# A Fourier filter in front of a gated feed-forward layer: inverse transforms of three y tiles in one unit instead of two

## The chip, the cores and the metric

The kernel runs on one core of one Trainium2 chip. Times are device microseconds (us) of one execution; the kernel before was run three times, and its time is the median of these.

## What is computed

A batch of 8 sequences (3008 tokens, 256 features, 32-bit floats) is filtered in frequency space, and each token then goes through a two-layer network with a hard-swish gate:

```python
X = np.fft.rfft(x, axis=1)                      # x: (8, 3008, 256)
Y = X * (filt_r + 1j * filt_i)[None]
y = np.fft.irfft(Y, n=3008, axis=1).reshape(24064, 256)
h = y @ w_in                                    # 256 -> 2048
g = h * np.clip(h + 3.0, 0.0, 6.0) / 6.0
out = g @ w_out                                 # 2048 -> 256
```

## The kernel before

**The network sets the rhythm.** Tokens are taken in 47 blocks of 512 (`k`), hidden features in 8 parts of 256 (`p`). One pair (k, p) is one **step**; step i is 8k + p, and there are 376. Both matrix products are done in Strassen's way with 7 products. In step i the loop emits the up product of (k, p) and, woven into it, the down product of the step before, (kd, pd):

1. `up_1`: three products into the PSUM banks `al` and `be`;
2. `do(0)`: the place for EARLY units of the transform;
3. `g_sums`: on VectorE (DVE), the second half of the gate of the step before (`hswish(.., 1)`, L737) and the sums L744, L745, L747; then down product 1;
4. `up_2`: two products. If pd is 0, `out_4` on DVE (L838, L839), which reads bank `po2` of the last block. Then `up_2b`: DVE adds h = be + s (L713), after which `be` is not used until the next step;
5. down products 2 and 4; if pd is 7, `out_1` (ScalarE, L820); `up_3`: one product into `al`, then DVE L718, which reads `al`; down products 5 and 6;
6. `up_4`: the first relu on ScalarE (L732); `do(1)`: the place for `w_scale`;
7. if pd is 0, `out_5` on DVE (L843), which reads bank `po3` of the last block; `hswish(.., 0)` on DVE (L737);
8. `up_5`: the last up product into `al`; ScalarE copies it (L727) and does the second relu (L732);
9. if pd is 7, `out_2` and `out_3` on DVE (L829, L834) around down products 7 and 3; `do(2)`: the place for all other units.

At p = 0 new `po` tiles are taken in the same four PSUM banks: in the step with pd = 0, down product 5 is the first that writes `po2`, and down product 7 the first that writes `po3`.

**The transform is threaded through the steps.** A batch n is transformed while the blocks before it go through the network. Its units are given to steps by hand, with lists in `places(n)`, and a unit's instructions run in the order of the code: each engine takes its instructions in this order (the schedule is manual). For n = 2 to 7 the steps are counted here from a base of 8·first[n] − 40, written as +j (first[n] is 11, 17, 23, 29, 35, 41):

- `a_unit` (L446): first transform, in +j below zero and again from +34 on for the next batch;
- `b_unit` (L493): second transform of two tiles, in both banks `psf`, at +2, +6, +12, +18, +22, +28, EARLY;
- `f_unit`: filter products, three DVE operations (L514 to L516), at +2, +3, +6, +7, +12, +13 and 16 steps later, in `do(2)`;
- `y_unit`: two DVE operations (L525, L526) that finish a y tile, at +4, +5, +10, +11, +14, +15 and 16 later, in `do(2)`; three buffers (`yp`);
- `bi_unit`: first inverse transform of two y tiles, EARLY, at +8, +14, +17, +24, +30, +33. Four products of 64 rows, 64 columns and 512 elements (L537), each on another quarter of the TensorE array, into the two banks of the pool `psF`; two ScalarE copies (L540) into `t3`; then `g_store`, two DMAs from the GpSimd queue (L553), in `do(2)`;
- `n_five` and `n_unit` (L627, L638): the last inverse transform, EARLY, most often at +1, +9, +16, +25; both banks of `psF`. ScalarE copies the tokens into `xn`, and after some of them `t_sums` on GpSimd (L683) makes the sums that the up product takes.

Each 32-bit product is two instructions in the records.

Of the kernel before, what the change touches and what calls it, by code (L numbers as in the profile page):

```python
# [10 lines left out]
FP32 = mybir.dt.float32  # L11
I32 = mybir.dt.int32
AXT = mybir.ActivationFunctionType
# [19 lines left out]
P = 128  # L33
D = 256
# [147 lines left out]
def kernel(  # L182
# [9 lines left out]
    nc = tc.nc  # L192
# [12 lines left out]
    g_d = nc.dram_tensor("g_tmp", (B, NC, 2, KH, D), FP32, kind="Internal").ap()  # L205
# [3 lines left out]
    def pool(name, bufs, **kw):  # L209
        return ctx.enter_context(tc.tile_pool(name=name, bufs=bufs, **kw))  # L210

    const = pool("const", 1)
    t1p = pool("t1p", 2)
# [3 lines left out]
    t3p = pool("t3p", T3B)  # L217
# [6 lines left out]
    psF = pool("psF", 2, space=PSUM)  # L224
    psU = pool("psU", 1, space=PSUM)
# [10 lines left out]
    wi = const.tile([P, 4, NC], FP32, name="wi")  # L236
# [10 lines left out]
    st = {}  # L247
# [282 lines left out]
    def bi_unit(b, i, ps=None):  # L530
        ys = [st.pop(("y", b, i + v)) for v in range(2)]
        ps = ps or [psF.tile([P, 2, D], FP32, name="psf", tag="f") for ri in range(2)]
        for v, ri in ((0, 0), (1, 0), (0, 1), (1, 1)):

            products = isinstance(ys[v], tuple)
            w, y = (wi[:, 1 + ri, :], ys[v][ri]) if products else (wi[ts(ri, 64), 0 if b else 3, :], ys[v][ts(ri, 64)])
            nc.tensor.matmul(ps[ri][ts(v, 64)], w, y, start=True, stop=True)  # L537
        t = (t3p if b or i & 2 else t1p).tile([P, 2, 2, D], FP32, name="t3" if b or i & 2 else "t1")
        for ri in range(2):
            nc.scalar.activation(out=t[:, ri, :, :], in_=ps[ri], func=AXT.Copy)  # L540
        st["t3", b, i] = t

    def g0_first(i):
        t = st["t3", 0, i]
        for v in range(2):
            for h in range(2):
                (nc.scalar, nc.sync)[v].dma_start(g_d[0, ds(h * HC + 1, NJ + 1), :, ds(2 * (i + v), 2), :].rearrange("c ri u d -> c ri (u d)"),
                                    t[ds(v * 64 + h * HC + 1, NJ + 1)].rearrange("p ri u d -> p ri (u d)"))
# [10 lines left out]
    for b in range(B):  # L559
# [4 lines left out]
        n = 0  # L564
# [106 lines left out]
    def xb(k, d, c):  # L671
        return xn[:, d, c, ts(k % 3, PAIRS)]
# [13 lines left out]
    def product(ps, p, w, x, start=False, stop=False):  # L686
        nc.tensor.matmul(ps, w_in[p][:, w, :], x, start=start, stop=stop, skip_group_check=True)  # L687
# [36 lines left out]
    def up_5(k, p):  # L724
        al = st["up"][0]
        product(al, p, A22, xb(k, 1, 1), stop=True)
        nc.scalar.activation(out=st["h"][1][:, 0:256], in_=al, func=AXT.Copy)  # L727
        relu(1)

    def relu(i):  # L730
        r = rp.tile([P, 512], FP32, name="r", tag="r")
        nc.scalar.activation(out=r, in_=st["h"][i], func=AXT.Relu, bias=half_c, scale=1.0 / 6.0)  # L732
        st["r", i] = r
# [56 lines left out]
    def plain_up(p):  # L790
        st["g", 0, p] = gp.tile([P, 7, 256], FP32, name="g")
        st["h"] = [psU.tile([P, 512], FP32, name=n) for n in ("al", "be")]
        for i in range(2):
            for d in range(2):
                nc.tensor.matmul(st["h"][i], w_in[p][:, 2 * d + i, :], xn[:, d, :, 0:PAIRS], start=d == 0, stop=d == 1)  # L795
            relu(i)
            hswish(0, p, i)

    def plain_down(p, tokens=(0, 1)):
        g = st["g", 0, p]  # L800
        if p == 0:
            st["po", 0] = [psO.tile([P, 2, 2, P], FP32, name="po%d" % i) for i in range(2)]
        for t in tokens:
            for u in range(2):
                for i, a in ((0, G11), (1, G12)):
                    nc.tensor.matmul(st["po", 0][t][:, u, :, :].rearrange("p a m -> p (a m)"), g[:, a + t, ts(u, P)],  # L806
                                     w_out[p][:, 2 * i:2 * i + 2, :].rearrange("p j m -> p (j m)"),
                                     start=p == 0 and u == 0 and i == 0, stop=p == NP - 1, skip_group_check=True)
# [50 lines left out]
    for b in range(B):  # L859
        for n, m, na in (((0, 6, NA), (6, 16, NA), (22, 9, NA)) if b == 0 else ((0, 16, NA), (16, 15, NA)) if b < B - 1  # L860
                         else ((0, 16, NA), (16, 10, NA), (26, 1, SPLIT))):
            o = b * HC * NA + n * NA
# [27 lines left out]
    plan = {}  # L890


    EARLY = (a_unit, b_unit, bi_unit, n_unit, n_five)

    def at(step, fn, *a):
        plan.setdefault((step, 0 if fn in EARLY else 1 if fn == w_scale else 2), []).append((fn, a))

    with tc.manual_schedule():

# [42 lines left out]
        ps = psU.tile([P, 512], FP32, name="al")  # L942
# [115 lines left out]
        def places(n):  # L1058
            if n == 1:
                return (list(range(2, NB + 2)), [12, 13, 15, 18, 19, 20, 22, 23, 26, 27, 28, 30],  # L1060
                        [14, 15, 16, 19, 21, 22, 24, 25, 27, 29, 30, 31], [16, 21, 24, 29, 31, 32])
            k = first[n] * NP
            a_at = [k - 7 * NP + i for i in (2, 4, 7, 9, 11, 13, 14, 15)]
            f_at, y_at, bi_at = ([k - (5 - 2 * r) * NP + i for r in range(2) for i in p]
                                 for p in ((2, 3, 6, 7, 12, 13), (4, 5, 10, 11, 14, 15), (8, 14, 17)))
            return a_at, f_at, y_at, bi_at

        at(n_at[TAIL - 2] + 1, lambda: nc.sync.dma_start(edge, wai_d[:, ds(NW + ND, ND)]))
# [2 lines left out]
        for n in range(1, B):  # L1071
            a_at, f_at, y_at, bi_at = places(n)
            for c, s in enumerate(a_at):
                at(s, a_unit, n, c)
                at(s, a_sums, n, c)
                at(s, z_store, n, c, nc.sync if n == 1 else nc.gpsimd)
                if c >= 3:
                    at(max(a_at[c - 3], s - 6), x_load, n, c)
                elif n > 1:
                    at(max(prev[c + NB - 3], s - 6), x_load, n, c)  # L1080
            for c in range(NT):
                s = f_at[2 * (c - TB) + (n == 1)] + 1 if c >= TB else a_at[-1] + 1
                at(s, t2_load, n, c)
                s = f_at[2 * (c - FB) + 1] + 1 if c >= FB else a_at[-1 if n > 1 else 3] + 1
                at(s, table_load, n, c)
            for i in range(NU):
                if i % 2 == 0 or n == 1:
                    at(f_at[i], b_unit, n, i)
                if i % 2 == 0:
                    at(bi_at[i // 2], bi_unit, n, i)  # L1090
                    at(bi_at[i // 2], g_store, n, i)
                at(y_at[i], y_unit, n, i)
            for i in range(NU):
                at(f_at[i], f_unit, n, i)
            prev = a_at
# [4 lines left out]
        for i in range(len(items) + 1):  # L1100
            up = i < len(items)
            k, p = items[min(i, len(items) - 1)]
            dn = i > 0
            kd, pd = items[i - 1]
            def do(place):
                for fn, a in plan.get((i, place), ()):
                    fn(*a)

            if k == 0:
                plain_up(p)  # L1110
                do(0)
                if dn:
                    plain_down(pd)
                do(1)
                do(2)
                continue
            if not up:
                last_down()
                break
            up_1(k, p)  # L1120
            ends = k == LAST and p == NP - 1
            do(0)
            last_plain = dn and kd == 0
            dn = dn and kd > 0
            if dn:
                g_sums(kd, pd)
                down(kd, pd, 1)
            if up:
                up_2(k, p)
            if dn and pd == 0 and kd > 1:  # L1130
                out_4(kd - 1)
            if up:
                up_2b(k, p)
            if dn:
                down(kd, pd, 2, 4)
                if pd == NP - 1:
                    out_1(kd)
            if up:
                up_3(k, p)
            if dn:  # L1140
                down(kd, pd, 5, 6)
            if up:
                up_4(k, p)
                do(1)
            if ends:
                out_1(k)
            if last_plain:
                plain_down(pd, (0,))
            if dn and pd == 0 and kd > 1:
                out_5(kd - 1)  # L1150
            if up:
                hswish(k, p, 0)
            if up:
                up_5(k, p)
            if last_plain:
                plain_down(pd, (1,))
                plain_out()
            if dn:
                if pd == NP - 1 or ends:
                    out_2(kd)  # L1160
                down(kd, pd, 7, 3)
                if pd == NP - 1 or ends:
                    out_3(kd)
            do(2)
# [30 lines left out]
```

## Time and profile before

| | us |
|---|---|
| median of 3 runs | 2660.61 (2660.59 to 2660.66) |
| the profiled execution's own time | 2658.29 |
| its span, first to last instruction | 2656.3 |
| PE busy | 2640.7 (99%) |
| DVE busy | 2053.4 (77%) |
| ScalarE (ACT) busy | 1318.7 (50%) |
| GpSimd (POOL) busy | 495.6 (19%) |

The views used are the page (busy time, the chain of work that ended last), the waits (who waited for whom), one engine's timeline (start and duration in us, engine, line, operation, out<-in, count, and in brackets the idle time before with what ended it) and the groups by line. PE is TensorE's matmuls, PEld its weight loads. A step is measured from the first matmul of its `up_1` to the next step's. All timelines are on the span's clock.

### The profile page before, as it was taken

How to read it: one execution, taken by the hardware profiler on the slowest of the kernel's cores; microseconds unless marked ns; L12 is line 12 of the kernel's file. 1: busy time of each engine (PE TensorE's matmuls, PEld its weight loads, DVE VectorE, ACT ScalarE, POOL GpSimd, SP SyncE). 2: the span in 40 equal slices, each digit the busy share in tenths (PEclk: the TensorE clock that was granted, in tenths of full speed). 3: DMA queues.
4: the chain of work that ended last, by engine and by line, in shares of the span. 5: the costliest groups of instructions: out<-in, count | busy, mean ns of one | idle time of the engine just before them, and what ended most of it. 6: DMA issues, size and time to landing. Idle time of an engine off the chain costs nothing.

```text
span 2656.3 us, 54240 instructions
## 1 busy us (share of the span) xinstructions
PE 2640.7 (99%) x21584; PEld 2316.5 (87%) x21584; DVE 2053.4 (77%) x3488; ACT 1318.7 (50%) x2688; POOL 495.6 (19%) x731
## 2 busy tenths in 40 slices
PE   9999999999999999999999999999999999999999
PEld 6688888888888888888888888888888888899998
DVE  7878868887688877888768887788877878766666
ACT  4554454555545554454544545545455454554554
POOL 2242021110311103111031210311113120111110
PEclk9999999999999999999999999999999999999999
DMA  9732233112241122411323113231122421110000
GB/s 251 216 91 74 68 96 105 56 36 81 79 109 56 36 83 76 109 56 37 87 72 109 56 40 85 70 109 56 49 77 70 109 59 50 42 43 21 20 20 24
DMA packets 134818, 198.24 MB, mean 75 GB/s; under 512 B 23146, under 2 KB 99016, under 8 KB 134374
## 3 DMA queue, kind: packets, MB, share of 16 engines
q1 hardware_dynamic: 117037, 150.12, 19.8%
q0 software_dynamic: 16960, 44.16, 6.3%
q8 instruction: 170, 2.79, 0.4%
q14 instruction: 82, 0.67, 0.1%
q10 hardware_dynamic: 569, 0.50, 0.1%
HBM read 122.43 MB, written 83.98 MB: 78 GB/s over the span
## 4 chain that ended last, share of the span: by engine, by line
PE 95%; DVE 2%; DMA 1%; issue 0%; ACT 0%; SPq 0%; POOL 0%; POOLq 0%; DVEq 0%; ACTq 0%
PE po L763 43%; PE al L687 24%; PE be L687 17%; PE psf L446 2%; PE psn L627 2%; PE psf L537 2%; PE psf L493 1%; PE po L806 1%; PE al L795 0%; PE be L795 0%; DMA w_all<-in_x_dram 0%; DVE g L737 0%; PE po L502 0%; DMA out_dram<-o 0%; PE psn L638 0%
## 5 line engine op out<-in xcount | busy, mean ns | idle before, releaser
L763 PEld LDWEIGHTS po<-w_all,g 128*128 128x128 f32 x10276 | 1362.1, 191 | 153.3 <-issue 44.5
L763 PE MATMUL po<-w_all,g 128*128 128x128 f32 x10276 | 1402.3, 276 | 0.1
L732 ACT ACTIVATE r<-h,half_c 128x512 f32<-128x512 f32 x736 | 532.9, 724 | 356.4 <-DVE h L713 344.5
L737 DVE SCALAR_TENSOR_TENSOR g<-r,h 128x512 f32<-128x512 f32 x736 | 531.3, 722 | 215.2 <-ACT r L732 203.2
L687 PE MATMUL al<-xt,w_all 128*128 128x256 f32 x2208 | 659.6, 381 | 0.1
L687 PE MATMUL be<-xt,w_all 128*128 128x256 f32 x1472 | 437.8, 379 | 0.0
L713 DVE TENSOR_TENSOR h<-be,s 128x512 f32<-128x512 f32 x368 | 253.8, 690 | 157.2 <-PE be L687 151.3
L687 PEld LDWEIGHTS al<-xt,w_all 128*128 128x128 f32 x2208 | 335.4, 192 | 1.0 <-issue 0.5
L687 PEld LDWEIGHTS be<-xt,w_all 128*128 128x128 f32 x1472 | 279.7, 190 | 37.9
L727 ACT ACTIVATE h<-al 128x256 f32<-128x256 f32 x368 | 141.7, 385 | 319.8 <-PE al L687 319.7
L718 DVE TENSOR_TENSOR h<-al,s 128x256 f32<-128x256 f32 x368 | 155.9, 424 | 149.6 <-PE al L687 148.5
L745 DVE TENSOR_TENSOR g<-g 128x512 f32<-128x512 f32 x367 | 261.7, 713 | 12.6
L708 ACT ACTIVATE s<-al 128x256 f32<-128x256 f32 x368 | 141.8, 385 | 194.6 <-PE al L687 191.2
L553 POOL DMA_DIRECT2D g_tmp<-t x96 | 55.4, 591 | 938.2 <-ACT t L540 926.2
L699 ACT ACTIVATE s<-be 128x256 f32<-128x256 f32 x368 | 141.7, 385 | 175.9 <-PE be L687 175.9
L687 PE MATMUL al<-xn,w_all 128*128 128x256 f32 x736 | 222.5, 384 | 1.4 <-DVE h L718 1.3
L687 PE MATMUL be<-xn,w_all 128*128 128x256 f32 x736 | 218.9, 379 | 0.0
L683 POOL TENSOR_TENSOR xt<-xn 128x256 f32<-128x256 f32 x184 | 136.7, 761 | 433.7 <-ACT xn L609 399.6
L744 DVE TENSOR_TENSOR g<-g 128x256 f32<-128x256 f32 x367 | 172.7, 471 | 12.5
L698 ACT ACTIVATE s<-al 128x256 f32<-128x256 f32 x368 | 141.8, 385 | 67.8 <-PE al L687 67.8
L747 DVE TENSOR_TENSOR g<-g 128x256 f32<-128x256 f32 x367 | 160.1, 436 | 12.5
L467 POOL DMA_DIRECT2D z_tmp<-t x192 | 95.3, 504 | 364.9 <-DVE t L460 347.5
(152 smaller groups left out, 1846.7 us busy)
## 6 DMA issues: line engine op xcount, KB each, us to landing
g_tmp<-t POOLq DMA_DIRECT2D x96, 256.0 KB, 3.7
t<-g_tmp SPq DMA_DIRECT2D x184, 120.0 KB
t<-z_tmp SPq DMA_DIRECT2D x42, 512.0 KB
z_tmp<-t POOLq DMA_DIRECT2D x192, 96.0 KB, 2.5
xs<-in_x_dram SPq DMA_DIRECT2D x112, 128.0 KB
o_tmp<-o SPq DMA_DIRECT2D x46, 256.0 KB
ft<-in_filt_r_dram SPq DMA_DIRECT2D x168, 64.0 KB
ft<-in_filt_i_dram SPq DMA_DIRECT2D x168, 64.0 KB
```

Of the source, the lines that this page charges most:

```text
L687: nc.tensor.matmul(ps, w_in[p][:, w, :], x, start=start, stop=stop, skip_group_check=True)
L698: nc.scalar.activation(out=s[:, 0, :], in_=al, func=AXT.Copy)
L699: nc.scalar.activation(out=s5, in_=be[:, 1, :], func=AXT.Copy)
L708: nc.scalar.activation(out=s[:, 1, :], in_=al, func=AXT.Copy)
L713: nc.vector.tensor_tensor(out=st["h"][0].rearrange("p (a n) -> p a n", a=2), in0=be, in1=s, op=ALU.add)
L718: nc.vector.tensor_tensor(out=st["h"][1][:, 256:512], in0=al, in1=s5, op=ALU.add)
L732: nc.scalar.activation(out=r, in_=st["h"][i], func=AXT.Relu, bias=half_c, scale=1.0 / 6.0)
L737: nc.vector.scalar_tensor_tensor(out=st["g", k, p][:, o:o + 2, :].rearrange("p a n -> p (a n)"), in0=st["r", i], scalar=1.0, in1=st["h"][i ...
L744: v.tensor_tensor(out=g[:, G1, :], in0=g[:, G3, :], in1=g[:, G22, :], op=ALU.add)
L745: v.tensor_tensor(out=g[:, G3:G2 + 1:2, :], in0=g[:, G3:G1 + 1, :], in1=g[:, G11:G11 + 1, :].broadcast_to([P, 2, 256]), op=ALU.subtract)
L747: v.tensor_tensor(out=g[:, G4, :], in0=g[:, G12, :], in1=g[:, G2, :], op=ALU.subtract)
L763: nc.tensor.matmul(st["po", k][bank][:, part, u, :], g[:, a, ts(u, P)], w_out[p][:, w, :], start=(p == 0 and n in OPENS and u == 0), stop= ...
```

## The change

For n = 2 to 7 a unit takes three y tiles instead of two. There are four such units in a batch, at +10, +17, +26 and +33, in place of six. `bi3_unit` is not EARLY: it is put in `do(1)`, after `up_4` and ahead of `out_5`, `hswish(.., 0)` and `up_5`. It has 12 products of 256 elements in three rounds of four, into the two banks of `psF` and the bank `be`, here called `c`. DVE copies `c` into `t3` in two pieces, 64 columns after the first round and 448 after the last; ScalarE copies one bank of `psF` in the unit and the other one after `up_5` (`bi3_copies`). `g3_store` issues four DMAs from the GpSimd queue instead of two. The y tiles +10 and +11 (and 16 later) come at +8 and +10. Batches 0 and 1 keep `bi_unit`.

```diff
@@ bi_unit @@
-        t = (t3p if b or i & 2 else t1p).tile([P, 2, 2, D], FP32, name="t3" if b or i & 2 else "t1")
+        t = t3p.tile([P, 3, 2, D], FP32, name="t3")[:, 0:2] if b or i & 2 else t1p.tile([P, 2, 2, D], FP32, name="t1")
...
+    def bi3_unit(b, i):
+        ys = [st.pop(("y", b, i + v)) for v in range(3)]
+        c = psU.tile([P, 512], FP32, name="be")
+        banks = [psF.tile([P, 512], FP32, name="psf", tag="f") for ri in range(2)]
+        t = t3p.tile([P, 3, 2, D], FP32, name="t3")
+        to = [t[:, q, :, :].rearrange("p u d -> p (u d)") for q in range(3)]
+        for r in range(3):
+            for v in range(2):
+                for ri in range(2):
+                    x, u, ps, o = (2, v, c, ri) if r == 2 * ri else (v, r - 1 + ri, banks[ri], r - 1 + ri)
+                    nc.tensor.matmul(ps[ts(v, 64), ts(o, D)], wi[ts(ri, 64), 0, :], ys[x][ts(ri, 64), u, :], start=True, stop=True)
+            if r == 0:
+                nc.vector.tensor_copy(out=to[2][:, 0:64], in_=c[:, 0:64])
+        nc.scalar.activation(out=to[1], in_=banks[1], func=AXT.Copy)
+        nc.vector.tensor_copy(out=to[2][:, 64:512], in_=c[:, 64:512])
+        st["t3", b, i] = t
+        st["bi3"] = to[0], banks[0]
+
+    def bi3_copies():
+        if "bi3" in st:
+            to, ps = st.pop("bi3")
+            nc.scalar.activation(out=to, in_=ps, func=AXT.Copy)
+
+    def g3_store(b, i):
+        t = st.pop(("t3", b, i))
+        for v in range(2):
+            nc.gpsimd.dma_start(g_d[b, :, :, ds(2 * (i + v), 2), :].rearrange("c ri u d -> c ri (u d)"),
+                                t[ts(v, 64), 0:2].rearrange("p ri u d -> p ri (u d)"))
+        for u in range(2):
+            nc.gpsimd.dma_start(g_d[b, :, :, 2 * (i + 2) + u, :], t[ts(u, 64), 2])
...
-        plan.setdefault((step, 0 if fn in EARLY else 1 if fn == w_scale else 2), []).append((fn, a))
+        plan.setdefault((step, 0 if fn in EARLY else 1 if fn in (w_scale, bi3_unit) else 2), []).append((fn, a))
...
-                                 for p in ((2, 3, 6, 7, 12, 13), (4, 5, 10, 11, 14, 15), (8, 14, 17)))
+                                 for p in ((2, 3, 6, 7, 12, 13), (4, 5, 8, 10, 14, 15), (10, 17)))
...
-                if i % 2 == 0:
+                if n == 1 and i % 2 == 0:
                     at(bi_at[i // 2], bi_unit, n, i)
                     at(bi_at[i // 2], g_store, n, i)
+                if n > 1 and i % 3 == 0:
+                    at(bi_at[i // 3], bi3_unit, n, i)
+                    at(bi_at[i // 3], g3_store, n, i)
...
             if up:
                 up_5(k, p)
+            bi3_copies()
```

## The prediction

> **What bounds the kernel now.** I read the page first: PE is busy 99%, and the chain of work that ended last is 95% PE.
>
> ```profile
> PE 2640.7 (99%) x21584; PEld 2316.5 (87%) x21584; DVE 2053.4 (77%) x3488; ACT 1318.7 (50%) x2688; POOL 495.6 (19%) x731
> PE 95%; DVE 2%; DMA 1%; issue 0%; ACT 0%; SPq 0%; POOL 0%; POOLq 0%; DVEq 0%; ACTq 0%
> ```
>
> So time is the sum of PE's steps: what PE issues, the turns between its full and its quartered array, and the moments in which DVE holds it. The timeline of PE gives each step's length, from one first `al<-xt` matmul to the next. A step without a unit takes 6.15 (1154.67 to 1160.82 below), and 169 steps are such. One with `bi_unit` takes 7.365 where nothing waits (1195.59 to 1202.95), so that unit costs 1.217; at +8, +14, +24, +30 it takes 7.45, as its second bank waits for L516 of the filter product before it.
>
> ```profile
> 1154.67 0.60 PE L687 MATMUL al<-xt,w_all 128*128 128x256 f32 x2
> ...
> 1160.82 0.38 PE L687 MATMUL al<-xt,w_all 128*128 128x256 f32 x1
> ...
> 1195.59 0.60 PE L687 MATMUL al<-xt,w_all 128*128 128x256 f32 x2
> 1196.98 1.09 PE L537 MATMUL psf<-y,wi 64*64 64x512 f32 x8
> 1202.95 0.38 PE L687 MATMUL al<-xt,w_all 128*128 128x256 f32 x1
> ```
>
> The waits view tells who holds PE. These rows are small, but each stands for a rule that the change will meet again.
>
> ```profile
> PEld al L687 <- DVE h L718: 3.7, 12, 0.7
> PEld po L763 <- DVE o L839: 1.2, 3, 0.5
> ```
>
> The last up product overwrites `al` and waits for L718 (+4). Down product 5 overwrites `po2` and waits for `out_4` (L839). The second is seen best in the step that begins at 192.95, in batch 1, after a step that had `out_2`, `out_3` and a y tile at its end. First DVE, then PEld:
>
> ```profile
> 193.15 0.42 DVE L834 TENSOR_TENSOR o<-po,o 128x256 f32<-128x256 f32 x1
> 193.59 0.69 DVE L525 TENSOR_TENSOR y<-s 64x512 f32<-64x512 f32 x1
> 194.31 0.69 DVE L526 TENSOR_TENSOR y<-s 64x512 f32<-64x512 f32 x1
> 195.10 0.69 DVE L737 SCALAR_TENSOR_TENSOR g<-r,h 128x512 f32<-128x512 f32 x1
> 197.01 0.86 DVE L747 TENSOR_TENSOR g<-g 128x256 f32<-128x256 f32 x1
> 198.13 0.41 DVE L839 TENSOR_TENSOR o<-po,o 128x256 f32<-128x256 f32 x1
> ...
> 198.59 0.97 PEld L763 LDWEIGHTS po<-w_all,g 128*128 128x128 f32 x8 [0.44 <-DVE o L839]
> ```
>
> DVE is 2.15 behind the step's start with its gate (L737), L839 ends at 198.54, and PE loads 0.05 later after 0.44 of idling; the step is 0.34 too long.
>
> **What the Trainium skill says.** "TensorEngine Tiling (Array Packing)", Key Properties: changing the tiling mode drains TensorE. The trace agrees: 0.33 of idle weight loading before each quartered unit. "PSUM — Partial Sum Buffer", PSUM bank collisions raise a hardware error: TensorE and another engine mustn't touch one bank in the same partitions at once, so a program has to order them, even for different columns; hence the third round's products in `c` must follow the 64-column copy. No row of before shows that. "SBUF — State Buffer", Who interferes with whom: a DVE operation with two SBUF inputs contends with GpSimd's reads. It does here: L744 takes 0.83 instead of 0.42 beside L683, L747 above 0.86.
>
> **The array's work.** *Removed*: 36 units. Twelve at 1.217, 24 at 1.217 plus their bank waits (step lengths less 6.148 and 1.217: 22 times about 0.09, once 0.13, once 0.26), 46.2 in all. *Added*: 24 units of 12 products. The nearest row is `a_unit`: 8 products of 256 elements on quarters, 1.221 a step, of which streaming is 4 rounds of 0.213 (half of a 256-element product's 0.43 in the timeline) and 0.37 the two turns. Six such rounds and one pair of turns give 1.65. The ordering in `c`: the first round's results come some 0.65 after the unit's start, the copy about 0.25 later (256 columns take 0.42, 512 take 0.69), the third round is due after 0.85; a delay of 0 to 0.2, I take 0.05. So 1.70 each, 40.8. Balance −5.4.
>
> **Stalls that lose their cover.** Two filter products in a row put the gate 1.47 behind its step; without a unit in the step this ends in a wait for L718, 0.20 at +4 and +20. At +8, +14, +24, +30 the removed unit hid the same. 24 × 0.20 = **+4.75**. In the other direction, the stalls at +10 and +26 (nine of them, 0.09 to 0.31, GpSimd beside DVE) lie before `up_5`, where the new unit now gives DVE time: **−2.0**.
>
> **y at +8 and +24.** These steps have pd = 7, so the y tile lies behind `out_2` and `out_3`, as in the step before 192.95: the gate will be some 2.2 late at +9 and +25. Where there is `n_five` and then GpSimd's L683 from 3.8 on (nine cases), I take that step's 0.35; without L683 (batch 7, +9) L839 just fits. At +25 of batches 6 and 7 there is no EARLY unit: L839 would end 2.2 + 2.99 = 5.19 into the step, the load is due at 3.72, so 1.45. 3.15 + 2.9 = **+6.05**.
>
> **y at +10 and +26.** The unit's weights begin 5.04 into the step (0.33 after the last up product's 4.71), its matmuls end at 6.6. The 448-column copy (the 512-column COPY of L457 took 0.68; 0.60) to 7.2, the gate's first half 0.7 and y 1.43 bring the next gate to 9.4, with the next step at 7.85: 1.54 late, where 1.27 is free (1.47 costs 0.20). 0.27 each, nine times (three have an EARLY unit at +11 or +27): **+2.4**. Their L698 waits for the second ScalarE copy and ends about where its product is due; nothing taken, 0.1 at most.
>
> **+17 and +33: two waits.** Both have pd = 0. (a) `out_4`: at +17 of five batches L683 slows DVE and L839 ends 4.27 into the step (4.36 once). The EARLY unit moved down 5's load from 3.72 to 4.94; at 3.72 it waits 0.6, a step of 0.53 (once 0.62): **+2.7**. At +33 L839 ends at 3.58, no wait. (b) `out_5` stands behind the copies of `c` on DVE, and the copies behind the unit's last matmul. The copy runs from 6.64, L843 from 7.16 to 7.57. Down 7, the first writer of `po3`, is due at 6.74 and loads at 7.62: 0.88, of which 0.07 is regained as at other late loads; 0.81. Queued behind it on PE: down 3 and all of the next step. Twelve times, **+9.7**. Bounds: 0.37 if only down 3 is held (0.44 later), 0.95 with a slower unit.
>
> **What costs nothing.** ScalarE's copies: in the unit it waits 1.65 longer for `up_5` than before and copies 0.6 in that time; the second copy is behind the second relu, in time that ScalarE (50% busy) has idle. Without that cover a copy would hold the next up product for 0.6. GpSimd issues four DMAs of about 0.59 instead of two per unit (16 for 12 per batch); `g3_store` waits for the late ScalarE copy, up to 1 us into the next step, and nothing follows it on GpSimd for steps. The first load of these results is issued at +35, two steps after +33, and used at +38; SP's queue is not otherwise moved. If the cover went, that load has some 20 us.
>
> **Sum**: −46.2 + 40.8 + 4.75 − 2.0 + 6.05 + 2.4 + 2.7 + 9.7 = **+18.2 us**. Against the profiled execution: span 2656.3 to 2674.5, its own time (2.0 more) 2658.29 to 2676.5. The median is 2.3 above that execution; so 2660.61 + 18.2 = 2678.8, slower by 0.7%.
>
> **Rivals.** *A, a smaller loss* (0.14): `out_5` holds down 3 alone, as it reads the other half of the bank. For: the halves are disjoint. Against: down 7 is the first writer of a newly taken tile, as down 5 is, and that waits for L839. 12 × 0.44 less: +12.9, 2673.5. *B, the saved turns decide* (0.20): DVE has 23% of idle time, and if it catches up before PE needs it, the holds (25.6 in my sum, 1.07 per new unit, all at DVE's readers of `al`, `po2`, `po3`) don't reach PE; with none of them −5.4 − 2.0 = −7.4, 2653.2. For: nearly all steps with pd = 0 in the trace run without a stall. Against: they do so under an EARLY unit or with nothing late on DVE; 192.95 and +4 show the holds. It decides from holds under 7.4, 0.31 per unit. *C, products not four at a time*, 24 × 0.213 plus turns, 5.5 per unit, +91: excluded by `a_unit`, the same quarters and banks.
>
> **How the numbers follow.** Forecast 0.66, A 0.14, B 0.20, of which 0.12 is faster by over 0.2% and 0.08 within 0.2% (5.3 us, about what a measurement here can tell from no change). Low end: A (−5.3), no stalls at +9 beside L683 (−3.2) nor at +11 and +27 (−2.4), units at 1.65 (−1.2): −12.1, 2667. High end: units at 1.85 (+3.6), holds of 0.95 (+1.7), +9 and +11 each 0.15 longer (+2.7): +8, 2687. B is left out.
>
> **What will show it.** In the profile after: steps +10 and +26 at 7.85 with a quartered unit of about 1.5; a wait of PEld po for `out_5`'s line, 12 times about 0.8 (that there is none would fell the largest term); one for `out_4`'s line, 16 times; waits for L718 at +8, +14, +24, +30 of 0.2. If PE's step at +33 is under 8.0, the forecast is wrong.

## The result, and the profile after

The changed kernel takes 2683.56 us (median of 4 runs, 2683.1 to 2683.86) beside 2660.64 for the kernel before on the same chip (4 runs, 2660.59 to 2661.08): **1.0086 times as long, 95% interval 1.0068 to 1.0103**, 22.9 us slower. The forecast was 2678.8, the range 2667 to 2687.

First the busy times and the chain of the changed kernel, in the lines that were shown of before:

```profile
PE 2649.7 (99%) x21872; PEld 2333.2 (87%) x21872; DVE 2071.1 (77%) x3536; ACT 1302.0 (49%) x2664; POOL 512.3 (19%) x755
PE 86%; DVE 9%; issue 2%; DMA 1%; ACT 1%; SPq 0%; DVEq 0%; POOL 0%; POOLq 0%; ACTq 0%
```

The busy share of PE is still 99%. What has moved is the chain: 9% of it is now DVE's, where it was 2%. So the lost time isn't found in busy times; one has to ask where PE waits for DVE. The waits view (who waited, for whom, us in total, times, longest) names three rows:

```profile
PEld po L794 <- DVE o L870: 11.6, 19, 1.1
PEld po L794 <- DVE o L874: 10.1, 12, 0.8
PEld al L718 <- DVE h L749: 6.3, 9, 1.7
```

All lines of the network lie 31 further down than in the kernel before: L718 is the up product (L687 before), L794 the down product, L749 the reader of `al` (L718 before), L768 the gate, L870 the second half of `out_4`, L874 `out_5`. The first row had 1.2 us in 3 waits before and has 11.6 in 19, 16 more, as forecast; the second is new, exactly the 12 waits that the prediction announced; the third had 3.7 in 12.

Now the same from the lengths of the steps, those of after less those of before. They add up to +21.9 us:

| | predicted | measured |
|---|---|---|
| 24 units of 1.77 for 36 of 46.2 in all | −5.4 (1.70 each) | −3.65 |
| stalls uncovered at +8, +14, +24, +30 | +4.75 | +4.96 |
| stalls hidden at +10, +26 | −2.0 | −2.03 |
| `out_4` late at +9, +25 | +6.05 | +7.7 |
| gate late at +11, +27 | +2.4 | +0.65 |
| `out_4` at +17, five times | +2.7 | +2.4 |
| `out_5` at +17, +33, 12 times | +9.7 | +8.5 |
| +27 of batches 6 and 7 | 0 (set apart, as an EARLY unit stands there) | +3.54 |
| other steps | 0 | −0.2 |
| the time behind TensorE's last product | 0 | +2.24 |

The two profiled executions differ by more than the medians do (own times 2683.85 and 2658.29): the profiled execution of before lies 2.3 below its median, and their starts, ahead of the first step, differ by 1.6, which varies from run to run (0.4 to 1.9 over all the runs below).

The largest term is seen in the step at +33 of batch 4. It begins at 1312.48. Timeline of DVE, then PE's, from the unit on:

```profile
1318.11 0.23 DVE L555 COPY t<-be 128x64 f32<-128x64 f32 x1 [1.07 <-PE be L553]
1319.11 0.62 DVE L557 COPY t<-be 128x448 f32<-128x448 f32 x1 [0.77 <-PE be L553]
1319.65 0.41 DVE L874 TENSOR_TENSOR o<-po,o 128x256 f32<-128x256 f32 x1
```
```profile
1317.40 0.13 PEld L553 LDWEIGHTS be<-y,wi 64*64 64x64 f32 x1
...
1318.39 0.43 PE L553 MATMUL be<-y,wi 64*64 64x256 f32 x1
...
1318.98 0.30 PEld L718 LDWEIGHTS al<-xn,w_all 128*128 128x128 f32 x2 [0.38 <-issue]
...
1320.11 0.97 PEld L794 LDWEIGHTS po<-w_all,g 128*128 128x128 f32 x8 [0.84 <-DVE o L874]
```

Read across the two: DVE does nothing from the first copy to the second but wait for the unit's last products (0.77 idle, released by L553). `out_5` (L874), ready long before, stands behind the second copy, ends at 1320.06, and 0.05 later down product 7 loads its weights after 0.84 without any. Of the unit itself one sees the third round: its product begins at 1318.39, 0.99 after the unit's first load, and 0.05 after the 64-column copy has ended (1318.11 + 0.23). The prediction had the third round due after 0.85 and took 0.05 of delay; it was 0.14.

The row that was sized worst lies in the step that begins at 1942.66, +27 of batch 6. Timeline, first GpSimd's sums beside DVE, then PE's load:

```profile
1943.34 0.69 DVE L526 TENSOR_TENSOR y<-s 64x512 f32<-64x512 f32 x1
...
1944.13 0.69 DVE L768 SCALAR_TENSOR_TENSOR g<-r,h 128x512 f32<-128x512 f32 x1
...
1946.05 2.59 DVE L778 TENSOR_TENSOR g<-g 128x256 f32<-128x256 f32 x1
1946.18 2.16 POOL L714 TENSOR_TENSOR xt<-xn 128x256 f32<-128x256 f32 x3
...
1949.16 0.41 DVE L749 TENSOR_TENSOR h<-al,s 128x256 f32<-128x256 f32 x1
...
1949.62 0.30 PEld L718 LDWEIGHTS al<-xn,w_all 128*128 128x128 f32 x2 [1.71 <-DVE h L749]
```

The y tile that now comes behind +26's unit (L525 and L526) puts the gate 1.47 behind its step, where the prediction had 1.54; in the other steps +11 and +27 that costs 0.07. But here DVE's last sum (L778, two inputs from SBUF, 0.42 to 0.43 when alone) comes just as GpSimd begins three sums in a row. It takes 2.59 and ends 0.3 after the last of the three. L749 stands behind it, and PE waits 1.71 for `al`. The sums themselves begin 3.5 into the step, where in the kernel before they began 2.24 into it: directly ahead of them in GpSimd's queue stand the four store issues of +26's unit, which end at 1946.23.

Last, a part of the profile that the prediction didn't look at: the drains with which each engine ends. The groups of the closing line, before and then after (minimum, median and maximum in ns):

```profile
L1190 POOLq DRAIN  x3: 40/102/4542, 2651.0 to 2656.1; - x3
```
```profile
L1225 POOLq DRAIN  x3: 40/93/6508, 2674.5 to 2681.8; - x3
```

In both kernels TensorE's last product ends 9.77 us after the last step begins. Behind it, GpSimd's drain takes 4.54 us before and 6.51 after, and the end comes 2.24 later.

### The profile page after: what moved, and what is told of

Same layout as the page of the kernel before. It is cut to its first block, busy times and chain, and to the rows that moved or that the text cites. A ratio compares the mean times of both kernels' runs of the same rounds, so it can differ in the third digit from the quotient of the medians.

```text
span 2682.1 us, 54885 instructions
## 1 busy us (share of the span) xinstructions
PE 2649.7 (99%) x21872; PEld 2333.2 (87%) x21872; DVE 2071.1 (77%) x3536; ACT 1302.0 (49%) x2664; POOL 512.3 (19%) x755
## 3 DMA queue, kind: packets, MB, share of 16 engines
q0 software_dynamic: 17344, 44.16, 6.2%
## 4 chain that ended last, share of the span: by engine, by line
PE 86%; DVE 9%; issue 2%; DMA 1%; ACT 1%; SPq 0%; DVEq 0%; POOL 0%; POOLq 0%; ACTq 0%
PE po L794 39%; PE al L718 21%; PE be L718 15%; PE psf L446 2%; DVE g L768 2%; PE psn L658 2%; PE psf L493 1%; DVE g L776 1%; PE po L837 1%; DVE h L744 1%; DVE g L775 1%; ACT r L763 1%; PE be L553 1%; PE psf L553 1%; PE psf L537 1%
## 5 line engine op out<-in xcount | busy, mean ns | idle before, releaser
L794 PEld LDWEIGHTS po<-w_all,g 128*128 128x128 f32 x10276 | 1362.1, 191 | 146.9 <-DVE g L775 18.8
L794 PE MATMUL po<-w_all,g 128*128 128x128 f32 x10276 | 1401.6, 276 | 10.2 <-DVE o L874 5.3
L768 DVE SCALAR_TENSOR_TENSOR g<-r,h 128x512 f32<-128x512 f32 x736 | 529.4, 719 | 220.4 <-ACT r L763 206.7
L718 PE MATMUL al<-xt,w_all 128*128 128x256 f32 x2208 | 659.6, 381 | 0.1
L718 PE MATMUL be<-xt,w_all 128*128 128x256 f32 x1472 | 437.8, 379 | 0.0
L718 PEld LDWEIGHTS al<-xt,w_all 128*128 128x128 f32 x2208 | 335.4, 192 | 1.0 <-issue 0.5
L718 PEld LDWEIGHTS be<-xt,w_all 128*128 128x128 f32 x1472 | 279.7, 190 | 37.9
L758 ACT ACTIVATE h<-al 128x256 f32<-128x256 f32 x368 | 141.4, 384 | 285.7 <-PE al L718 285.6
L776 DVE TENSOR_TENSOR g<-g 128x512 f32<-128x512 f32 x367 | 261.3, 712 | 12.6
L749 DVE TENSOR_TENSOR h<-al,s 128x256 f32<-128x256 f32 x368 | 155.3, 422 | 114.6 <-PE al L718 113.5
L718 PE MATMUL al<-xn,w_all 128*128 128x256 f32 x736 | 227.8, 391 | 4.6 <-DVE h L749 4.5
L718 PE MATMUL be<-xn,w_all 128*128 128x256 f32 x736 | 218.9, 379 | 0.0
L775 DVE TENSOR_TENSOR g<-g 128x256 f32<-128x256 f32 x367 | 173.2, 472 | 12.5
L778 DVE TENSOR_TENSOR g<-g 128x256 f32<-128x256 f32 x367 | 165.6, 451 | 12.5
L718 PEld LDWEIGHTS be<-xn,w_all 128*128 128x128 f32 x736 | 139.8, 190 | 18.9
```

The source lines that it names most:

```text
L749: nc.vector.tensor_tensor(out=st["h"][1][:, 256:512], in0=al, in1=s5, op=ALU.add)
L768: nc.vector.scalar_tensor_tensor(out=st["g", k, p][:, o:o + 2, :].rearrange("p a n -> p (a n)"), in0=st["r", i], scalar=1.0, in1=st["h"][i ...
L775: v.tensor_tensor(out=g[:, G1, :], in0=g[:, G3, :], in1=g[:, G22, :], op=ALU.add)
L776: v.tensor_tensor(out=g[:, G3:G2 + 1:2, :], in0=g[:, G3:G1 + 1, :], in1=g[:, G11:G11 + 1, :].broadcast_to([P, 2, 256]), op=ALU.subtract)
L778: v.tensor_tensor(out=g[:, G4, :], in0=g[:, G12, :], in1=g[:, G2, :], op=ALU.subtract)
L794: nc.tensor.matmul(st["po", k][bank][:, part, u, :], g[:, a, ts(u, P)], w_out[p][:, w, :], start=(p == 0 and n in OPENS and u == 0), stop= ...
```

## The experiments

**My theory**: the loss is not in the units but in DVE's queue. The unit sits where TensorE has no slack, and what DVE has to do ahead of `out_4`, `out_5` and L749 comes too late: the copies of the third bank at +17 and +33, the y tile that was moved to +8, the one at +10. The **rivals**: that `out_5` holds only the small down product 3 (A of the prediction); that three-tile units are costly wherever they stand; that the place ahead of the last up product costs by itself.

### `out_5` ahead of the unit

```diff
                 up_4(k, p)
+                if dn and pd == 0 and kd > 1:
+                    out_5(kd - 1)
                 do(1)
...
-            if dn and pd == 0 and kd > 1:
-                out_5(kd - 1)
```

> out_5 is issued ahead of the three-tile unit, so that on VectorE it no longer stands behind the two copies of bank c; nothing else is changed. Theory (what is queued behind the copies on VectorE holds TensorE): the wait of down product 7 for out_5 goes in all 12 steps +17 and +33, which were 0.71 us too long each: 8.5 us less than the changed kernel, 2675.1, and step +33 takes 7.92 instead of 8.63. Rival (the unit itself, its place or its transfers cost the time, in whatever order VectorE works): no change, 2683.6.

Measured: 2675.93 beside 2659.44 for the kernel before (ratio 1.0062, 1.0047 to 1.0077). The steps are 8.56 shorter than the changed kernel's: +17 and +33 lose 0.71 each, in all six batches, and nothing else moves. The waits for L874 are gone from the list of waits. Moving one instruction in DVE's queue takes away the largest term. That the hold is of down product 7, and not of down product 3 alone, is seen from the trace of after: the load waits 0.84 ahead of all eight weights of the two products, and a step loses 0.71, not the 0.37 of rival A. So A is out.

### The y tile of +8 at +9

```diff
-                                 for p in ((2, 3, 6, 7, 12, 13), (4, 5, 8, 10, 14, 15), (10, 17)))
+                                 for p in ((2, 3, 6, 7, 12, 13), (4, 5, 9, 10, 14, 15), (10, 17)))
```

> The third y tile of each group is made at +9 and +25 instead of +8 and +24, so it is not behind out_2 and out_3. Theory: the waits of down product 5 for out_4 at +9 and +25 go (0.49 in nine steps, 1.59 in two, 0.08 in one: 7.7 us), but in nine steps the y tile now reads SBUF beside GpSimd's sums, and the gate of +10 and +26 comes about 1.9 late, which holds down product 2 for some 0.25 each: 5.4 us less than the changed kernel in all, 2678.2 (2675.9 if nothing comes back). Rival (these steps are long because of the last inverse transform and GpSimd, wherever the y tile is): 2683.6.

Measured: 2684.16 (1.0094, 1.0079 to 1.0109), no gain at all; the steps are 0.06 longer than the changed kernel's. The cause is confirmed and the size of its return is missed. All of the 7.7 us at +9 and +25 are gone (those steps are back at 7.66 and 6.15, as before the change), so the y tile at +8 is what made `out_4` late. But +10 and +26 are longer by 0.74 to 0.94 in nine cases. The step at +10 begins at 1156.30 in this kernel; DVE's timeline there:

```profile
1155.97 1.11 DVE L525 TENSOR_TENSOR y<-s 64x512 f32<-64x512 f32 x1
1157.11 1.10 DVE L526 TENSOR_TENSOR y<-s 64x512 f32<-64x512 f32 x1
1158.32 1.03 DVE L768 SCALAR_TENSOR_TENSOR g<-r,h 128x512 f32<-128x512 f32 x1
```
```profile
1159.41 0.97 PEld L794 LDWEIGHTS po<-w_all,g 128*128 128x128 f32 x8 [0.74 <-DVE g L768]
```

Behind +9's tokens GpSimd makes its sums, and each half of the y tile takes 1.10 beside them instead of 0.69, the gate 1.03 instead of 0.69. The gate ends at 1159.35, and the down products that read it load 0.06 later. The y tile had been put in the one step whose end GpSimd occupies.

### The y tile of +10 at +11

```diff
-                                 for p in ((2, 3, 6, 7, 12, 13), (4, 5, 8, 10, 14, 15), (10, 17)))
+                                 for p in ((2, 3, 6, 7, 12, 13), (4, 5, 8, 11, 14, 15), (10, 17)))
```

> The fourth y tile is made at +11 and +27 instead of +10 and +26, where the unit's copies are. Theory: VectorE is on time at +11 and +27; the waits there go (0.07 in nine steps), and in batches 6 and 7 the subtraction L778 of +27 is done before GpSimd's sums begin, so that it no longer takes 2.59 us beside them (steps 1.79 and 1.75 too long): 4.2 us less than the changed kernel, 2679.4. Rival (at +27 it is GpSimd's sums that come later or last longer, for the stores of g): 3.5 of it stays, 2682.9.

Measured: 2681.12 (1.0083, 1.0068 to 1.0098); the steps are 2.48 shorter than the changed kernel's, where 4.2 were expected. +11 and +27 are back at their lengths of before, 6.15 and 6.60: the 0.07 nine times and the 1.79 and 1.75 of batches 6 and 7 all go. So the y tile behind the unit is the cause of both, and the 2.59 of L778 is no accident of one run. Not foreseen: in batches 6 and 7 the steps +28, +29 and +30 get 0.14, 0.43 and 0.23 longer: the tile now stands beside GpSimd's sums at the end of +27, and each half of it takes 1.10.

### The copies of the third bank on ScalarE

```diff
-                nc.vector.tensor_copy(out=to[2][:, 0:64], in_=c[:, 0:64])
+                nc.scalar.activation(out=to[2][:, 0:64], in_=c[:, 0:64], func=AXT.Copy)
...
-        nc.vector.tensor_copy(out=to[2][:, 64:512], in_=c[:, 64:512])
+        nc.scalar.activation(out=to[2][:, 64:512], in_=c[:, 64:512], func=AXT.Copy)
```

> ScalarE makes both copies of bank c instead of VectorE. Theory: VectorE is free of them, so out_5 holds nothing (8.5 us), the y tile behind the unit isn't late (0.65) and L778 meets no sums of GpSimd (3.5); ScalarE's copy of the last up product and its second relu come 0.2 to 0.3 later, which costs up to 0.1 at +11 and +27: some 11.5 us less than the changed kernel, 2672. Rival (bank c has to be emptied before the step can go on, by whichever engine): no gain, 2683.6 or more.

Measured: 2671.07 (1.0048, 1.0031 to 1.0064). The steps are 12.63 shorter: 0.71 at each +17 and +33, the 0.07 at +11 and +27, and 3.5 at +27 of batches 6 and 7. DVE around the unit of +33 of batch 4, where that step begins at 1307.45:

```profile
1311.59 0.42 DVE L749 TENSOR_TENSOR h<-al,s 128x256 f32<-128x256 f32 x1
1311.93 0.41 DVE L874 TENSOR_TENSOR o<-po,o 128x256 f32<-128x256 f32 x1
1312.42 0.69 DVE L768 SCALAR_TENSOR_TENSOR g<-r,h 128x512 f32<-128x512 f32 x1
```
```profile
1314.27 1.08 PEld L794 LDWEIGHTS po<-w_all,g 128*128 128x128 f32 x8
```

`out_5` ends before the unit has begun, and down product 7 loads without a wait. ScalarE takes all four copies of a unit. Against the changed kernel no step gets longer in more than one batch (one at +15 by 0.17), and ScalarE's copy of the last up product (L758) still ends 0.31 before the next step, as in steps without a unit. "PSUM — Partial Sum Buffer", Engine vs sequencer instructions, says that the queues of ScalarE, VectorE and GpSimd are strictly first in, first out. This run and the one with `out_5` first agree: the same `out_5` makes its step 0.71 longer or not at all, according to what stands ahead of it.

### Two-tile units at the new place

```diff
-        plan.setdefault((step, 0 if fn in EARLY else 1 if fn == w_scale else 2), []).append((fn, a))
+        plan.setdefault((step, 1 if fn == w_scale or fn == bi_unit and a[0] > 1 else 0 if fn in EARLY else 2), []).append((fn, a))
```

This is an edit of the kernel before.

> The kernel before, its two-tile units unchanged (products, ScalarE copies, places +8, +14, +17 and 16 later), but for batches 2 to 7 issued where the change puts its own: behind the gate and the down products before it, ahead of the last up product. If the loss comes from what the new unit is made of (two VectorE copies ahead of out_5 in the queue, y tiles at +8), and not from the place, this costs what two moved waits cost and no more: about as before, 2660.6, within 3 us. The rival, that the place itself costs, since the unit now stands between the two up products and every wait of TensorE behind it is uncovered: 36 units by some 0.2 us, 2668 or more.

Measured: 2667.08 (1.0027, 1.0016 to 1.0038), 7.5 slower than before. My expectation misses by 6.5; the rival's 0.2 a unit is nearly found, though not for its reason. The steps are 7.15 longer. At +17 of five batches `out_4` has lost the EARLY unit that hid it (2.5 in all). The unit itself is 0.09 shorter at +8, where it takes 1.09 instead of 1.18, since its bank is free; yet the steps with a unit are no shorter there and 0.09 longer at +33, and each step behind a unit is 0.10 longer (36 times). The trace shows where this comes from. At +8 of batch 4 first ScalarE, then PE, which begins the next step:

```profile
1143.62 1.09 ACT L540 ACTIVATE t<-psf 128x512 f32<-128x512 f32 x2 [0.75 <-PE psf L537]
1144.59 0.39 ACT L727 ACTIVATE h<-al 128x256 f32<-128x256 f32 x1
```
```profile
1145.04 0.70 PE L687 MATMUL al<-xt,w_all 128*128 128x256 f32 x2
```

ScalarE's two copies of the unit now stand ahead of L727, which reads the last up product out of `al`, and the next step overwrites `al`. It begins 0.05 after L727's end behind all 36 units, where in the kernel before it begins 0.31 after it. So it is again a queue, this time ScalarE's: 0.19 a unit. No run with the copies split was made of this kernel. In the changed kernel one copy stands ahead of L758, and at +10 and +26 the next step begins 0.31 after L758's end; so its 1.77 has nothing of this wait, and no cost of the place by itself is seen.

### Other places for the units

From the kernel with scalar copies; the y tiles go back to their places of before, so the units move on by a step or more.

```diff
-            f_at, y_at, bi_at = ([k - (5 - 2 * r) * NP + i for r in range(2) for i in p]
-                                 for p in ((2, 3, 6, 7, 12, 13), (4, 5, 8, 10, 14, 15), (10, 17)))
+            f_at, y_at = ([k - (5 - 2 * r) * NP + i for r in range(2) for i in p]
+                          for p in ((2, 3, 6, 7, 12, 13), (4, 5, 10, 11, 14, 15)))
+            bi_at = [k - 5 * NP + i for i in (11, 20, 27, 33)]
```

> The change with both copies of its third bank on ScalarE, with the y tiles back at their places of before (+4, +5, +10, +11, +14, +15) and the four units at +11, +20, +27 and +33. My theory: what is left of the loss after the scalar copies is the moved y tiles (+9, +25: about 7.7 us) and the uncovered stalls (+8, +14, +24, +30: 5.0). The first goes, so: 3.65 saved in units, 5.0 of stalls kept, about 1 us of stalls hidden at +20, and the sum is about as before, 2659.7. The rival, that three-tile units are costly wherever they stand: 2668 or more.

Measured: 2663.76 (1.0017, 1.001 to 1.0023). The 7.7 us at +9 and +25 are gone (7.66 and 6.15 again), so the rival falls, yet the expectation is missed by 4. Two terms were forgotten: `out_4` waits at +17 in five batches (6.67 instead of 6.15, 2.6 in all), since there is no unit ahead of it, and the end behind TensorE's last product is 1.95 longer than before. −0.9 + 2.6 + 1.95 = +3.65; measured are 4.1.

### The filter products and y tiles moved out of each other's way

```diff
-                          for p in ((2, 3, 6, 7, 12, 13), (4, 5, 10, 11, 14, 15)))
+                          for p in ((2, 3, 5, 7, 12, 14), (4, 6, 10, 11, 13, 15)))
```

> The kernel above (scalar copies, units at +11, +20, +27, +33) with two f units and two y tiles of each half moved by a step (f at +2, +3, +5, +7, +12, +14, y at +4, +6, +10, +11, +13, +15), so that the steps at +8, +14, +24 and +30 have none of the work that stalls there. My theory: the stalls that the removed units had hidden go too, and the three-tile unit's 3.65 us show: about 2655.4, 0.2% faster than before. The rival, that each step in which VectorE has a y tile has its own wait: no better than the kernel above, about 2660.

Measured: 2659.64 beside 2659.62 (0.9999, 0.9991 to 1.0008), as fast as before. +8, +14, +24 and +30 are at 6.15 to 6.17 in place of 6.34: the stalls of two filter products in a row are gone, and no step has taken them over. The steps are 2.53 shorter than those of the kernel before, and the end is 1.96 longer. The 2655.4 that I expected is missed by 4.2, by what had been forgotten above as well: `out_4` at +17 (2.6) and the end. The rival's number is met, but not its reason, since no step took over a wait.

### A shorter first copy

```diff
-                nc.vector.tensor_copy(out=to[2][:, 0:64], in_=c[:, 0:64])
+                nc.vector.tensor_copy(out=to[2][:, 0:16], in_=c[:, 0:16])
...
-        nc.vector.tensor_copy(out=to[2][:, 64:512], in_=c[:, 64:512])
+        nc.vector.tensor_copy(out=to[2][:, 16:512], in_=c[:, 16:512])
```

> The changed kernel with 16 columns instead of 64 in the first copy of the third bank, and 496 instead of 448 in the second. If the third round of the products waits for that copy, and the unit is 1.77 us instead of 1.70 for it, each of 24 units gains some 0.04 us (copies of 64 and 256 columns take 0.23 and 0.41, so 48 columns are worth 0.045), and each second copy takes 0.045 more, which out_5 and so the down product at +17 and +33 waits for (12 of them): -1.1 + 0.5, 2683. The rival, that the 1.77 is the matrix unit's own: 2684.1, only the second part.

Measured: 2682.72 beside 2659.62 (1.0086, 1.0073 to 1.01). The total is too near to tell. The steps tell: +10 and +26 are 0.05 shorter in all 12 cases, +17 and +33 not at all (what the unit gains there, the longer second copy takes from `out_5`), nine of the steps behind them give 0.05 back, and +27 of batch 7 is 1.14 shorter: DVE is 0.04 later there, so that GpSimd's sums begin while L776 still runs; L776 takes 1.22 instead of 0.69, and L778 0.83 instead of 2.55. So the third round does wait for the first copy, at the price expected. "TensorEngine Tiling (Array Packing)", Gotcha 1: PSUM Pressure, says that different row tiles can't access the same PSUM bank at once and that software has to keep them apart. This is presumably what the copy is for: round 1 writes `c` from one half of the rows, round 3 from the other. A kernel without that order wasn't tried, so no run here shows the rule itself, only what the order costs: 0.14 us a unit with 64 columns, about 0.09 with 16.

### The third tile's stores from another queue

```diff
-            nc.gpsimd.dma_start(g_d[b, :, :, 2 * (i + 2) + u, :], t[ts(u, 64), 2])
+            nc.sync.dma_start(g_d[b, :, :, 2 * (i + 2) + u, :], t[ts(u, 64), 2])
```

> The changed kernel with the two stores of each third tile (48 in all) issued by SyncE instead of GpSimd. The changed kernel's tail is 2.24 us longer than that of before, with TensorE's last product at the same place in it; GpSimd's closing drain takes 6.51 us instead of 4.54, and GpSimd issues 314 DMAs instead of 290. My theory: the drain grows with the number of DMAs that GpSimd has issued, by 1.97/24 = 0.082 us each. With 266 it takes about 2.6, and the tail gets shorter until SyncE's own last waits set the end, 2.7 earlier than GpSimd's did: 2683.56 - 2.7 = 2680.9, with the steps unchanged. The rival, that the drain is longer for something else in the change, or that it differs from run to run: drain 6.5, time 2683.5.

and, as an edit of the kernel before, all 72 stores of its inverse tiles in batches 2 to 7:

```diff
-            nc.gpsimd.dma_start(g_d[b, :, :, ds(2 * (i + v), 2), :].rearrange("c ri u d -> c ri (u d)"),
+            (nc.sync if b > 1 else nc.gpsimd).dma_start(g_d[b, :, :, ds(2 * (i + v), 2), :].rearrange("c ri u d -> c ri (u d)"),
```

> The kernel before with the 72 stores of its inverse tiles in batches 2 to 7 issued by SyncE instead of GpSimd, which keeps 218 DMAs. By the theory of the drain (0.082 us for each DMA issued) GpSimd's closing drain becomes short, under 1 us, and SyncE's own last waits set the end, 0.7 us earlier than GpSimd's does in the kernel before: 2658.9. The rival, that the drain has nothing to do with that number: drain 4.5, 2659.6, or later if loads wait behind the stores in SyncE's queue.

Measured: 2683.33 beside 2659.47 (1.0091, 1.0076 to 1.0107) for the first, 2663.70 (1.0016, 1.0009 to 1.0023) for the second. The closing drains of GpSimd, first and second kernel:

```profile
L1225 POOLq DRAIN  x3: 40/102/3121, 2675.4 to 2679.7; - x3
```
```profile
L1190 POOLq DRAIN  x3: 40/93/8557, 2652.6 to 2661.7; - x3
```

In the first the drain shrinks to 3.12 and the end comes 3.03 earlier, as expected, but next to nothing of it is seen in the median, since the steps are 2.0 longer (+27 of batches 6 and 7, 0.8 each, and +9 of batch 7, 0.36). At +27 of batch 6, a step that begins at 1941.50 in this run, one sees why:

```profile
1943.69 2.59 DVE L775 TENSOR_TENSOR g<-g 128x256 f32<-128x256 f32 x1
1943.83 2.16 POOL L714 TENSOR_TENSOR xt<-xn 128x256 f32<-128x256 f32 x3
```

With two issues fewer ahead of them GpSimd's sums begin 2.33 into the step instead of 3.5. Now they catch L775, the first of DVE's three sums, which takes 2.59, and the other two run beside the sums that follow (1.10 and 0.83). In the second, with the fewest DMAs from GpSimd, the drain is longest, 8.56; the steps are as before (+0.2), the end comes 4.0 later, and that is its whole loss of 4.2. **My theory of the drain falls.** What stands: kernels with the same number of packets in GpSimd's queue have the same drain (16960 packets, 4.54 in two kernels; 17344, 6.50 or 6.51 in eight; 15040, 3.12 and 3.15 in two), but the drain doesn't grow with that number (11200 packets, 8.56). By what rule stays open.

### All that helped, together

From the kernel with moved filter products: the two stores above from SyncE, 16 columns in the first copy, and

```diff
-            f_at, y_at = ([k - (5 - 2 * r) * NP + i for r in range(2) for i in p]
-                          for p in ((2, 3, 5, 7, 12, 14), (4, 6, 10, 11, 13, 15)))
+            f_at = [k - 5 * NP + i for i in (2, 3, 5, 7, 12, 14, 17, 19, 21, 23, 28, 30)]
+            y_at = [k - (5 - 2 * r) * NP + i for r in range(2) for i in (4, 6, 10, 11, 13, 15)]
```

> The kernel with scalar copies, moved units and retimed tiles, with three edits more: the third tiles' stores issued by SyncE (2.7 us off the tail, as above), the f units of the second half a step earlier at first (+17, +19, +21, +23, +28, +30), so that a filter unit, which is issued ahead of out_4, stands at +17 and hides the wait for out_4 there (five times 0.5), and 16 columns instead of 64 in the first copy (24 times 0.045). If these add up: 2659.6 - 2.7 - 2.5 - 1.1 = 2653.3, faster than before by 0.24%. The rival, that a filter unit at +17 only moves the wait to another step: 2655.8.

Measured: **2653.89** (16 runs, 2652.76 to 2655.57) beside 2659.47: ratio 0.9978, 0.9971 to 0.9986. It beats both kernels, by 5.6 us and by about 29. The terms add up: +17 and +18 together are 0.42 shorter in five batches, each unit 0.04, and the end is 2.66 earlier than that of the kernel it came from. How much of the gain is the three-tile unit's own isn't shown, as the same retiming wasn't tried with two-tile units. An estimate from the lengths: 36 units of 1.217 without bank waits are 43.8, 24 of 1.73 are 41.5, so some 2.3 of the 5.6. Its page and its waits:

```profile
PE 2636.8 (99%) x21872; PEld 2333.8 (88%) x21872; DVE 2050.4 (77%) x3488; ACT 1315.1 (50%) x2712; POOL 480.1 (18%) x707
PE 95%; DMA 3%; DVE 1%; issue 0%; ACT 0%; SPq 0%; POOL 0%; POOLq 0%; DVEq 0%; ACTq 0%
```
```profile
PEld al L718 <- DVE h L749: 3.0, 11, 0.5
PEld po L794 <- DVE o L870: 1.2, 3, 0.5
```

DVE is down to 1% of the chain, the row for `out_5` is gone, and that for `out_4` is back at its 3 waits and 1.2 us of the kernel before.

## Why the prediction held, step by step

**Bound and direction: right.** PE stayed the bound, and the time is the sum of its steps. The array's own gain was forecast at 5.4 and is 3.65, and the holds of DVE are a multiple of it; rival B, that DVE would catch up in its idle 23%, had a price per new unit of 1.07 against a limit of 0.31. Measured, the holds of the table add up to 27.7, 1.16 a unit.

**The unit** was mis-sized, 1.70 for 1.77. The term that failed is the wait in `c`, taken as 0.05: it is 0.14, as the third round's first product in `c` follows the copy's end by 0.05, which shows only in the trace of after. The rest of the model (six rounds of four and two turns, 1.65) fits within 0.02.

**Stalls uncovered and hidden**: right, 4.96 for 4.75 and −2.03 for −2.0. Both were read in steps of before that had the same work and no unit; that is the firmest kind of row.

**y at +8**: right in cause (the run with it at +9 takes it all away) and small by a fifth. Where `n_five` stands in the step, the wait cost 0.49, not the 0.35 of the step in batch 1. GpSimd is not the reason, as DVE's last sum takes 0.83 beside it here and took 0.86 there; DVE comes later out of the step before (`out_3` begins 0.37 into the step, there 0.20), and the gate is 2.32 behind in place of 2.15; at +9 of batch 7 it was 0.08 where I had none, and at +25 of batches 6 and 7 it was 1.59, not 1.45.

**y at +10**: right in cause, wrong in both sizes. The ordinary case cost 0.07, not 0.27: the gate was about as late as predicted (1.47 for 1.54), but the free limit of 1.27 that I had from +4 doesn't hold for these steps; the same 1.47 costs 0.20 there and 0.07 here. Of the difference 0.12 lies in one place: the addition behind DVE's last sum begins 0.46 after that sum's start at +4, in all batches, and 0.34 after it in the nine cases here; why is open. The case that I had set apart at no cost because of its EARLY unit, +27 of batches 6 and 7, cost 1.77 each, because of the sums of GpSimd that begin as L778 does: the tokens of that very unit are what they sum. "SBUF — State Buffer", Who interferes with whom, calls the port pair that VectorE and GpSimd share an exclusive lock, and I had cited it; but I used it only as a factor on durations (0.83 for 0.42, which is also measured). L778's 2.59 beside three sums in a row shows that such a lock can last for a burst: it ended 0.3 after the last of them, though its record begins 0.13 before the first (starts on GpSimd are rough in these traces).

**+17 and +33**: right. The hold by `out_5` was forecast at 0.81 and is 0.71, 12 times as said. The unit's first load comes 4.92 into the step, not 5.04, but its second copy (from 6.63), `out_5` and the load behind it (7.63) lie as the working has them; the load waits 0.84, and 0.13 of that, not 0.07, is regained. `out_4` at +17: 0.48 for 0.53.

**What was costed at nothing** is where the prediction failed outright. Of `g3_store` it said that nothing follows it on GpSimd for steps. At +27 of batches 6 and 7 GpSimd's sums stand right behind its four issues and begin 3.5 into the step instead of 2.24, with L778. And something follows all of GpSimd's DMAs, the drain at the end of the kernel: it is 1.97 longer and the end 2.24 later, by a rule that stayed open. Without it the measured sum would be within 4 of the forecast; with it the total lies 4.8 above the forecast, and inside the range, whose high end was built from other terms. To that extent the number is luck: the unit's 1.75, the 3.54 at +27 and the end's 2.24 came on top, and the terms for +11, `out_4` at +17 and `out_5` were 3.3 too high.

## What to carry to other kernels

When a unit with its own copies is put into a full queue, don't ask only whether the copying engine has idle time, but what stands behind the copies in its queue and who waits for that: two copies in each of 12 units, in the wrong queue, cost 8.5 us here, and the same copies in a queue with room for them cost none. Room has to be looked at each time: on ScalarE the copies of the two-tile units at the late place cost 0.19 a unit, for what stood behind them. Moving work out of one step's way puts it into another's; look first at which steps the neighbour on a shared port is busy in. And compare the ends of the two traces as well as the middle, for 2 to 4 us were lost there with no instruction of the change near.

## What the runs showed of the hardware that I had not expected

- A DVE sum of two SBUF inputs whose record begins with a burst of GpSimd sums, or up to 0.14 us before it, was held for the whole burst: 2.59 us instead of 0.42 beside three sums of 2.16 in all (L778 in the changed kernel; L775 with the stores moved). Beside sums that were already running it took 0.83, and 512-element ones 1.10 instead of 0.69.
- GpSimd's drain at the end of the kernel took from 3.12 to 8.56 us, with the same value for the same number of packets in its queue, and neither rising nor falling with that number.
- Two 64-row halves of the array that write one PSUM bank in turn, with a copy between them, cost 0.14 us a unit with a copy of 64 columns, 0.05 less with 16; the product behind the copy started 0.05 after its end.
